# One planned list of steps for an attention stage, with four blocks of the next matrix product placed among the steps

## The chip, the cores and the metric

The kernel runs on one core of one Trainium2 chip. The metric is the device time of one execution in microseconds (us). It is given as the median of several runs. One more execution was recorded by the hardware profiler, and every row below comes from that one.

The engines carry short names. PE is TensorE, whose matmuls and weight loads (PEld) overlap. DVE is VectorE, ACT is ScalarE, POOL is GpSimd, and SP is SyncE, which here only issues DMAs. Each engine runs its own instructions in the order in which they were written, and waits at an instruction whose inputs or buffers are not ready.

## What is computed

The reference is a causal attention followed by two feed-forward layers:

```python
scores = (q @ k^T) / sqrt(64)            # batch 2, heads 12, seq 448, head_dim 64
scores = where(mask, -1e9, scores)
attn = exp(scores - max); attn /= sum(attn) + 1e-9
x = (attn @ v) as [896, 768]
h = x @ w_in                             # 768 -> 2048
g = h if h >= 1, 0 if h <= -1, else (h + 1)**2 / 4
x = g @ w_out                            # 2048 -> 768
...                                      # then one of 8 experts per token: relu(x @ w1[e]) @ w2[e], gated
```

`w_in` and `w_out` come as 64-bit floats, and the kernel turns them into 32-bit ones on the chip.

## The kernel before

**Stages.** The 24 heads are worked on as 12 pairs, pairs 0 to 5 for batch 0 and pairs 6 to 11 for batch 1. Each pair fills one of the six 128-row pieces of `xh["x", b]` and `xl["x", b]`, the high and low part of the attention's output. Then comes the first layer (`gemm1`): 16 blocks `m` of 128 output features, for two batches. A block is six triples of matmuls (`mm3`, L102 to L104), so 18 matmuls of 448 columns. The second layer (`gemm2`) and an expert follow, built from the same triples.

**Steps of a pair.** `m` is the head of the pair (0 or 1) and `i`, `j` a block of 112 rows or columns.

- S (`t_S`, L178, PE): scores of block `i`, one matmul for each head, into two "s" banks of PSUM.
- K (`t_K`, L194, DVE): adds the mask and takes the row maximum.
- E (`t_E`, L198, ACT): exponential with row sums.
- SUM (`t_SUM`, L205 and L206, DVE): the reciprocal of the row sums, for both heads at once.
- N (`t_N`, L211, POOL): multiplies a block by the reciprocal.
- F (`t_F`, L221, PE): transposes of 112x112, four, three or three of them into a "t" bank.
- T (`t_T`, L228, ACT): copies that bank to SBUF.
- V (`t_V`, L235, PE): probabilities times values, into the "x" bank.
- XH and XL (L242, L246, DVE): high part, and low part, of the pair's output.

**Order.** `ORDER` is a table for one turn of a loop. `S:3@0` is a step of the turn's own pair, `T:21@2` one of the pair two turns back. The loop runs 15 turns, so in the last ones fewer and fewer pairs have steps left. `FILL` and `PREP` put work of the first layer among the last turns: three blocks of batch 0 (`EARLY = 3`) and the preparation of their weights.

**Preparing a weight** (`from64` and `work`, tiles of 128x768): Abs on ACT (L92), four DVE operations, called Z1 (L93), Z2 (L95), C1 (L96) and C2 (L98) here, then the high part H on ACT (L132) and the low part L on POOL (L133). In `gemm1` this goes on beside the matmuls, two weights ahead (`Ahead.step`). What follows a block's matmuls is `act1`: a clip on DVE (L272), a square on ACT (L273), a maximum on DVE (L275), a high part on ACT and a low part on POOL.

**Buffers.** [...] The raw weights have two buffers, the raw q and k three.

Of the kernel before, what the change touches and what calls it, by code (L numbers as in the profile page):

```python
# [28 lines left out]
SIGN = 0x80000000  # L29
# [2 lines left out]

ORDER = [(t.split("@")[0], int(t.split("@")[1])) for t in """
    SUM@1 XL@3 F:00@2 S:3@0 S:2@0 K:31@0 N:30@1 K:30@0 K:20@0 T:21@2 T:01@2 N:20@1 F:10@2 T:00@2 K:21@0 E:31@0
    E:30@0 N:10@1 E:20@0 F:11@2 E:21@0 F:20@1 V:0@2 V:2@2 T:11@2 S:1@0 S:0@0 K:11@0 N:31@1 K:10@0 V:3@2 T:10@2
    K:00@0 T:20@1 E:11@0 E:10@0 N:21@1 K:01@0 V:1@2 N:01@1 E:00@0 N:11@1 XH@2 F:21@1 F:01@1 E:01@0 N:00@1
""".split()]
VB = 3 + max(lag for _, lag in ORDER)  # L40
LAST_V = max((lag, n, int(t[2:])) for n, (t, lag) in enumerate(ORDER) if t[:1] == "V")[2]

FILL = {(1, 'F:11'): 3, (1, 'V:1'): 3}
PREP = {(-1, 'F:10'): 1, (-1, 'V:0'): 1, (-1, 'F:21'): 1, (0, 'F:00'): 1, (0, 'F:11'): 1, (0, 'V:0'): 1, (0, 'V:1'): 1, (1, 'F:00'): 1, (1, 'F:11'): 1}
EARLY = 3
BANKS = {"s": 4, "t": 3, "x": 1}
CYCLE = "ststsxst"


def f32(ap):  # L50
    return ap.bitcast(F32)
# [3 lines left out]
def routed_block(ctx, tc, qk, v, w_in, w_out, w_g, w1, w2, out):  # L55
    nc = tc.nc
# [104 lines left out]

    at = ExitStack()
    aq = at.enter_context(tc.tile_pool(name="aq", bufs=2))
    raw_qk, val, hilo, pr, pt, px, pss, pst = {}, {}, {}, {}, {}, {}, {}, {}

    def t_load(p):
        raw_qk[p] = aq.tile([P, 2, S], F32, tag="qk", name="qk", bufs=3)
        nc.sync.dma_start(raw_qk[p], qk[p])
        val[p] = aq.tile([C, 2, NB, D], F32, tag="v", name="v", bufs=VB)
        nc.sync.dma_start(val[p], v[p])  # L170
# [7 lines left out]
            pe.matmul(ps[:, :w], raw_qk[p][r, 0, C * i:w], raw_qk[p][r, 1, :w], start=True, stop=True)  # L178

    def stats(p):  # L180
        if p not in pr:
            pr[p] = (
                [aq.tile([C, TRI[NB]], F32, tag="pr", name="pr", bufs=6) for m in range(2)],
                aq.tile([C, 2, NB], F32, tag="nm", name="nm", bufs=4),
                aq.tile([C, 2, NB], F32, tag="sm", name="sm", bufs=4),
            )
        return pr[p]
# [60 lines left out]
    STEPS = {n[2:]: f for n, f in locals().items() if n.startswith("t_")}  # L248

    def evac(ps, a, c):  # L250
        act.copy(a, ps)
        dve.tensor_tensor(c, ps, f32(a), op=ALU.subtract)


    def new_g(pool_, b, q):
        for hl, d in (("h", gh), ("l", gl)):
            d[b, q] = pool_.tile([P, 4, S], F32R, tag=f"g{hl}{b}{q}", name=f"g{hl}")

    def g_of(d, b, k):
        return d[b, k // 4][:, k % 4]  # L260

    def gemm1(m, b, wt, ps):

        wh, wl = wt
        for k in range(KD):
            mm3(ps, wh[:, k], wl[:, k], xh["x", b][:, k], xl["x", b][:, k], k == 0, k == KD - 1)
            yield

    def act1(m, b, ps, step):

        u = ga.tile([P, S], F32, tag="u", name="u")
        dve.tensor_scalar(u, ps, -1.0, 1.0, op0=ALU.max, op1=ALU.min)  # L272
        act.activation(u, u, AF.Square, bias=half, scale=0.5)  # L273
# [186 lines left out]
    ws = Ahead(win + wout)  # L460

    with tc.manual_schedule():
        dve.memset(half, 0.5)
# [12 lines left out]
        for q in range(1):
            new_g(g0, 0, q)
        N = NP

        held, banks = [], []  # L480

        def early():

            for m in range(EARLY):
                while not ws.ready:
                    ws.step(EARLY)
                held.append(ws.take())
                banks.append(bank("s"))
                yield from gemm1(m, 0, held[m], banks[m])

        fill = early()
        t_load(0)
        t_load(1)
        for s in range(N + max(lag for _, lag in ORDER)):
            if s + 2 < N:
                t_load(s + 2)
            for name, lag in ORDER:
                if 0 <= s - lag < N:
                    step, _, at_ = name.partition(":")
                    STEPS[step](s - lag, *(int(c) for c in at_))  # L500
                    for _ in range(FILL.get((s - N, name), 0)):
                        next(fill, None)
                    for _ in range(PREP.get((s - N, name), 0)):
                        ws.step(EARLY - len(held))
            if s == 2:
                load_gates()
            if s == N - 4:
                ws.load()
        for _ in fill:
            pass  # L510
# [131 lines left out]
```

## Time and profile before

| | |
|---|---|
| median of 3 runs | 480.35 us (480.21 to 480.82) |
| the profiled execution's own time | 480.02 us |
| its span, first to last instruction | 478.0 us |
| mean granted TensorE clock | 0.984 |
| busy: PE, DVE, ACT, POOL | 459.4, 266.5, 195.4, 199.7 us |
| the chain that ended last | PE 91%, DVE 4%, POOL 2%, ACT 1%, DMA 1% |

A matmul's end is modelled, and matmuls overlap in the pipeline. A PE that is shown busy is therefore not a PE at its best pace. How many instructions it starts in a stretch says more, and so does the granted clock beside it. The difference between the execution's time and its span, 2.0 us, is taken as fixed.

### The profile page before, as it was taken

How to read it: one execution, taken by the hardware profiler on the slowest of the kernel's cores; microseconds unless marked ns; L12 is line 12 of the kernel's file. 1: busy time of each engine (PE TensorE's matmuls, PEld its weight loads, DVE VectorE, ACT ScalarE, POOL GpSimd, SP SyncE). 2: the span in 40 equal slices, each digit the busy share in tenths (PEclk: the TensorE clock that was granted, in tenths of full speed). 3: DMA queues.
4: the chain of work that ended last, by engine and by line, in shares of the span. 5: the costliest groups of instructions: out<-in, count | busy, mean ns of one | idle time of the engine just before them, and what ended most of it. 6: DMA issues, size and time to landing. Idle time of an engine off the chain costs nothing.

```text
span 478.0 us, 6657 instructions
## 1 busy us (share of the span) xinstructions
PE 459.4 (96%) x2422; PEld 389.8 (82%) x2422; DVE 266.5 (56%) x538; ACT 195.4 (41%) x455; POOL 199.7 (42%) x190
## 2 busy tenths in 40 slices
PE   5999999679999999999999999999999999999995
PEld 3666565448889999999999999999978999999994
DVE  3576776843699999999947648366111441111111
ACT  4689889742445545545323223232132322211100
POOL 1645654761457677686514133141141222232210
PEclk9999999769999999999999999999999999999999
DMA  6332270240232432322315324150032110123311
GB/s 190 103 117 84 92 248 1 66 133 0 67 123 77 132 114 84 133 80 96 123 55 177 88 89 141 40 171 1 11 122 66 35 55 25 64 82 107 100 60 43
DMA packets 13093, 43.00 MB, mean 90 GB/s; under 512 B 1600, under 2 KB 3264, under 8 KB 13056
## 3 DMA queue, kind: packets, MB, share of 16 engines
q1 hardware_dynamic: 13056, 42.52, 27.6%
q8 instruction: 21, 0.34, 0.3%
q14 instruction: 16, 0.13, 0.1%
HBM read 39.76 MB, written 2.75 MB: 89 GB/s over the span
## 4 chain that ended last, share of the span: by engine, by line
PE 91%; DVE 4%; POOL 2%; ACT 1%; DMA 1%; issue 0%; DVEq 0%; ACTq 0%
PE ps L102 12%; PE ps L104 12%; PE ps L103 12%; PE pt L102 9%; PE pt L104 9%; PE pt L103 9%; PE ps L178 7%; PE pt L221 5%; PE px L235 5%; PE px L103 3%; PE px L104 3%; PE px L102 3%; DVE ps L194 1%; POOL pr L211 1%; DVE wc L98 1%; POOL wlo L133 1%
## 5 line engine op out<-in xcount | busy, mean ns | idle before, releaser
L133 POOL TENSOR_TENSOR wlo<-wc,whi 128x768 fp32r<-128x768 f32 (+1 forms) x34 | 67.6, 1987 | 108.5 <-ACT whi L132 70.5
L133 POOL TENSOR_TENSOR wlo<-wraw,whi 128x512 fp32r<-128x512 f32 (+1 forms) x20 | 30.2, 1513 | 92.0 <-ACT whi L132 80.3
L211 POOL TENSOR_SCALAR pr<-pr,sm 112x224 f32<-112x224 f32 (+2 forms) x96 | 50.5, 547 | 42.7 <-DVE sm L206 42.6
L277 POOL TENSOR_TENSOR gl<-u,gh 128x448 fp32r<-128x448 f32 x32 | 50.7, 1598 | 15.6 <-ACT gh L276 15.6
L102 PE MATMUL ps<-xh,whi 128*128 128x448 f32 x150 | 55.8, 372 | 0.0
L104 PE MATMUL ps<-xh,wlo 128*128 128x448 f32 x150 | 55.3, 368 | 0.4 <-POOL wlo L133 0.4
L103 PE MATMUL ps<-xl,whi 128*128 128x448 f32 x150 | 55.3, 369 | 0.0
L198 ACT ACTIVATE pr<-ps,nm 112x448 f32<-112x448 f32 (+3 forms) x96 | 46.5, 510 | 16.4 <-DVE nm L194 12.6
L194 DVE CUSTOM_DVE_ANT_0 ps<-ps,mask 112x448 f32<-112x448 f32 (+3 forms) x96 | 40.3, 481 | 23.1 <-PE ps L178 23.1
L132 ACT CAST whi<-wc 128x768 fp32r<-128x768 f32 (+1 forms) x34 | 27.2, 799 | 60.6 <-DVE wc L98 59.8
L96 DVE TENSOR_SCALAR wc<-wc 128x768 f32<-128x768 f32 (+1 forms) x34 | 44.4, 1306 | 0.8
L221 PEld LDWEIGHTS pt<-ident,pr 112*112 112x112 f32 x240 | 26.6, 148 | 20.1 <-POOL pr L211 9.9
L178 PE MATMUL ps<-qk 64*112 64x448 f32 (+3 forms) x192 | 37.6, 489 | 5.0 <-DMA qk<-qk 4.0
L273 ACT ACTIVATE u<-u,half 128x448 f32<-128x448 f32 x32 | 21.4, 669 | 48.0 <-DVE u L272 48.0
L95 DVE SCALAR_TENSOR_TENSOR wz<-wraw,wz 128x768 uint32<-128x768 uint32 (+1 forms) x34 | 40.2, 1182 | 0.6
L221 PE MATMUL pt<-ident,pr 112*112 112x112 f32 x240 | 33.1, 291 | 7.0 <-POOL pr L211 7.0
L102 PE MATMUL pt<-xh,whi 128*128 128x448 f32 x102 | 37.4, 367 | 0.0
L104 PE MATMUL pt<-xh,wlo 128*128 128x448 f32 x102 | 37.4, 366 | 0.0
L103 PE MATMUL pt<-xl,whi 128*128 128x448 f32 x102 | 37.3, 366 | 0.0
L98 DVE SCALAR_TENSOR_TENSOR wc<-wc,wz 128x768 uint32<-128x768 uint32 (+1 forms) x34 | 36.4, 1069 | 0.7
L178 PEld LDWEIGHTS ps<-qk 64*112 64x112 f32 x192 | 21.0, 196 | 17.8 <-ACT pr L198 5.7
L102 PE MATMUL ps<-gh,whi 128*128 128x448 f32 x96 | 35.3, 368 | 0.0
(159 smaller groups left out, 972.9 us busy)
## 6 DMA issues: line engine op xcount, KB each, us to landing
wraw<-w_in SPq DMA_DIRECT2D x16, 768.0 KB, 4.4
wraw<-w_out SPq DMA_DIRECT2D x12, 640.0 KB, 4.0
qk<-qk SPq DMA_DIRECT2D x12, 448.0 KB, 3.8
wraw<-w_out SPq DMA_DIRECT2D x6, 768.0 KB, 4.6
wraw<-w SPq DMA_DIRECT2D x8, 384.0 KB, 3.0
wraw<-w SPq DMA_DIRECT2D x12, 256.0 KB, 2.5
v<-v SPq DMA_DIRECT2D x12, 224.0 KB, 4.0
out<-res SPq DMA_DIRECT2D x11, 224.0 KB, 2.0
```

The costliest lines, as they stand in the source:

```text
L96: dve.tensor_scalar(c, c, 2.0**-31, None, op0=ALU.max)
L98: dve.scalar_tensor_tensor(cu, cu, 3, z, op0=ALU.logical_shift_left, op1=ALU.bitwise_xor)
L102: pe.matmul(ps, wh, xh, start=start, stop=False)
L103: pe.matmul(ps, wh, xl, start=False, stop=False)
L104: pe.matmul(ps, wl, xh, start=False, stop=stop)
L133: pool.tensor_tensor(fl, v, f32(fh), op=ALU.subtract)
L178: pe.matmul(ps[:, :w], raw_qk[p][r, 0, C * i:w], raw_qk[p][r, 1, :w], start=True, stop=True)
L194: dve.tensor_tensor_reduce(z, z, mask[:, S - w:], -0.125, 3.0e38, ALU.add, ALU.min, nm[:, m, i:i + 1])
L198: act.activation(q[m][:, TRI[i]:TRI[i + 1]], pss.pop((p, i, m))[:, :C * (i + 1)], AF.Exp, bias=nm[:, m, i:i + 1], scale=-1.0, accum_out=sm ...
L211: pool.tensor_scalar(r, r, sm[:, m, i:i + 1], 0.0, op0=ALU.mult, op1=ALU.add)
L221: pe.transpose(ps[:, o:o + C], q[:, TRI[i] + C * j:TRI[i] + C * j + C], ident[:C, :C])
L277: pool.tensor_tensor(g_of(gl, b, m), u, f32(g_of(gh, b, m)), op=ALU.subtract)
```

## The change

1. `ORDER` is now one list of every step of every pair, run once from first to last. `S2/7` is step S of block 2 for pair 7; `G1.4` is triple 4 of block 1 of the first layer.
2. Four blocks of the first layer for batch 0 (`EARLY = 4`) stand in the list as single triples `Gm.k`. Each `Gm.k` needs pair `k` only. Six triples make a block. All four blocks use one new PSUM bank "f", and "t" has two banks instead of three.
3. The weights of these four blocks are prepared in halves of 384 columns by steps of the list: A (Abs, ACT), Z1, Z2, C1, C2 (DVE), H (ACT), L (POOL). The first two prepared weights lie in the space of `g` tiles that are needed late (`hold`). The raw weights are loaded by the steps LW.
4. The clip, square, maximum, high and low part of these four blocks are steps too: U1 (DVE), SQ (ACT), U2 (DVE), GH (ACT), GL (POOL).
5. SUM is done for each head by itself.
6. The gates' weights are loaded after the first layer instead of in the third turn of the attention.

```diff
-ORDER = [(t.split("@")[0], int(t.split("@")[1])) for t in """
-    SUM@1 XL@3 F:00@2 S:3@0 S:2@0 K:31@0 N:30@1 K:30@0 K:20@0 T:21@2 T:01@2 N:20@1 F:10@2 T:00@2 K:21@0 E:31@0
...
-FILL = {(1, 'F:11'): 3, (1, 'V:1'): 3}
...
-EARLY = 3
-BANKS = {"s": 4, "t": 3, "x": 1}
-CYCLE = "ststsxst"
+ORDER = """
+    LQ/0 LW/0 S2/0 S3/0 K21/0 LQ/1 K20/0 E21/0 K30/0 E20/0 K31/0 E30/0 S1/0 E31/0 K11/0 LW/1 K10/0 E11/0 Z11/0
...
+    V3/11 XH/11 GH/3 XL/11 GL/3
+""".split()
+EARLY, HOLD, SPARE, VB = 4, 2, 4, 5
+BANKS = {"s": 4, "t": 2, "x": 1, "f": 1}
+CYCLE = "stsfstsx"
...
-    def t_SUM(p):
-        sm = pr[p][2]
+    def t_SUM(p, _, m):
+        sm = sms[p][:, m]
         dve.tensor_scalar_add(sm, sm, 1e-9)
         dve.reciprocal(sm, sm)
...
+    def t_A(j, h):
...
+        act.activation(ec[j][:, E * h:E * (h + 1)], words(j, h)[1].bitcast(F32), AF.Abs, scale=2.0**-16)
+
+    def t_Z(j, n, h):
+        low, high = words(j, h)
+        if n == 1:
...
+            dve.tensor_scalar(ez[j, h], low, 29, SIGN, op0=ALU.logical_shift_right, op1=ALU.bitwise_xor)
+        else:
+            z = ez[j, h]
+            dve.scalar_tensor_tensor(z, high, SIGN, z, op0=ALU.bitwise_and, op1=ALU.bitwise_xor)
+
+    def t_C(j, n, h):
+        c = ec[j][:, E * h:E * (h + 1)]
+        if n == 1:
+            dve.tensor_scalar(c, c, 2.0**-31, None, op0=ALU.max)
+        else:
+            cu = c.bitcast(U32)
+            dve.scalar_tensor_tensor(cu, cu, 3, ez.pop((j, h)), op0=ALU.logical_shift_left, op1=ALU.bitwise_xor)
...
+    def t_G(m, k):
+        if k == 0:
+            ebank[m] = bank("f" if m < SPARE else "s")
+        wh, wl = held[m]
+        mm3(ebank[m], wh[:, k], wl[:, k], xh["x", 0][:, k], xl["x", 0][:, k], k == 0, k == KD - 1)
...
-        t_load(0)
-        t_load(1)
-        for s in range(N + max(lag for _, lag in ORDER)):
...
+        for token in ORDER:
...
+            STEPS[name](*([] if p is None else [int(p)]), *args)
+        ws.load()
         at.close()
...
-        for m in range(EARLY):
-            act1(m, 0, banks[m], lambda: None)
         for m in range(KF):
...
+                    ahead = 1 if m < HOLD else 2
+                    act1(m, b, ps, lambda: ws.step(ahead))
...
+        load_gates()
```

**PE at the end of the attention.** The order before, from the transposes of pair 10 on (`pt<-ident,pr` is F, `px<-pt,v` is V, `xh,whi` the first layer):

```order
L221 MATMUL pt<-ident,pr 112x112 x20
L235 MATMUL px<-pt,v 64x448 x2
L235 MATMUL px<-pt,v 64x224 x2
L235 MATMUL px<-pt,v 64x112 x2
L235 MATMUL px<-pt,v 64x336 x2
L221 MATMUL pt<-ident,pr 112x112 x17
L102 MATMUL ps<-xh,whi 128x448
L103 MATMUL ps<-xl,whi 128x448
L104 MATMUL ps<-xh,wlo 128x448
```

The same place now, from the last transposes of pair 10 (`pf` is the new bank):

```order
L251 MATMUL pt<-ident,pr 112x112 x4
L133 MATMUL pf<-xh,whi 128x448
L134 MATMUL pf<-xl,whi 128x448
L135 MATMUL pf<-xh,wlo 128x448
L251 MATMUL pt<-ident,pr 112x112 x3
L266 MATMUL px<-pt,v 64x448 x2
L266 MATMUL px<-pt,v 64x224 x2
L266 MATMUL px<-pt,v 64x336 x2
L266 MATMUL px<-pt,v 64x112 x2
L251 MATMUL pt<-ident,pr 112x112 x3
L133 MATMUL pf<-xh,whi 128x448
L134 MATMUL pf<-xl,whi 128x448
```

Before, 37 transposes and the V of pair 10 stood ahead of the first triple. Now a triple stands after every three to four transposes, down to pair 11's own.

**DVE early in the attention.** The order before, from one SUM on (`ps,nm<-ps,mask` and `nm` are the two records of one K):

```order
L205 TENSOR_SCALAR sm<-sm 112x8
L206 RECIPROCAL sm<-sm 112x8
L246 TENSOR_TENSOR xl<-px,xh 128x448
L194 ISA ps,nm<-ps,mask 112x448
L194 ISA nm 112x1
L194 ISA ps,nm<-ps,mask 112x448
L194 ISA nm 112x1
```

The place now, in the steps around pair 2:

```order
L236 RECIPROCAL sm<-sm 112x4
L315 SCALAR_TENSOR_TENSOR wc<-wc,ez 128x384
L273 CAST xh<-px 128x448
L222 ISA ps,nm<-ps,mask 112x224
L222 ISA nm 112x1
L222 ISA ps,nm<-ps,mask 112x224
L222 ISA nm 112x1
L304 TENSOR_SCALAR ez<-wraw 128x384
L222 ISA ps,nm<-ps,mask 112x112
L222 ISA nm 112x1
```

Halves of the weights' preparation (`wc`, `ez`) now stand between the K steps, in front of steps for which ACT and then PE wait.

## Rows read from the trace of the kernel before

**Rows 1.** Windows: us, busy by engine, then clock, DMA share, GB/s; the attention's end.

```profile
84.00:96.00 12.00, 8.03 (x55) 5.69 (x55) 10.58 (x28) 8.21 (x25) 8.98 (x11) 0.78 0.21 67
96.00:108.00 12.00, 8.61 (x40) 5.90 (x37) 5.03 (x7) 5.57 (x11) 7.59 (x7) 0.65 0.42 131
```

**Rows 2.** Windows, the columns of rows 1: attention, first layer, expert.

```profile
24.30:82.36 58.06, 58.06 (x446) 35.52 (x445) 42.10 (x173) 51.17 (x188) 30.53 (x64) 1.00 0.34 112
132.00:228.00 96.00, 96.00 (x469) 87.87 (x470) 89.73 (x105) 49.53 (x78) 69.51 (x40) 1.00 0.32 105
...
432.00:456.00 24.00, 24.00 (x120) 22.24 (x119) 3.12 (x5) 3.11 (x5) 6.46 (x5) 1.00 0.31 103
```

**Rows 3.** Chain that ended last: start, us, what; one full pair.

```profile
47.92 1.50 PE ps L178 x8
49.43 1.01 PE pt L221 x9
50.43 1.28 PE px L235 x8
51.71 0.89 PE ps L178 x7
52.60 1.01 PE px L235 x8
53.61 1.20 PE pt L221 x11
54.81 1.50 PE ps L178 x8
```

**Rows 4.** Waits of PE: us in total, times, longest.

```profile
PE pt L221 <- POOL pr L211: 7.0, 4, 4.0
PE ps L104 <- POOL wlo L133: 0.4, 1, 0.4
```

**Rows 5.** Timeline of PE at the attention's end: start, us, instruction.

```profile
110.70 0.47 PE L102 MATMUL ps<-xh,whi 128*128 128x448 f32 x1
```

**Rows 6.** Chain that ended last, the start: pairs 1 and 2.

```profile
10.30 3.38 PE ps L178 x8
18.71 2.89 PE ps L178 x8
21.60 1.43 PE pt L221 x9
```

**Rows 7.** Groups of ACT by form, 82 to 110 us: busy, mean ns, idle before.

```profile
L92 ACT ACTIVATE wc<-wraw 128x768 f32<-128x768 f32 x3 | 2.8, 942 | 0.0
L132 ACT CAST whi<-wc 128x768 fp32r<-128x768 f32 x3 | 2.5, 833 | 3.2 <-DVE wc L98 3.2
```

**Rows 8.** Groups of DVE by form, 82 to 110 us: busy, mean ns, idle before.

```profile
L95 DVE SCALAR_TENSOR_TENSOR wz<-wraw,wz 128x768 uint32<-128x768 uint32 x3 | 3.2, 1065 | 0.0
L98 DVE SCALAR_TENSOR_TENSOR wc<-wc,wz 128x768 uint32<-128x768 uint32 x3 | 2.9, 965 | 0.1
L93 DVE TENSOR_SCALAR wz<-wraw 128x768 uint32<-128x768 uint32 x3 | 2.0, 652 | 0.0
L96 DVE TENSOR_SCALAR wc<-wc 128x768 f32<-128x768 f32 x3 | 1.6, 545 | 0.0
```

**Rows 9.** The same groups, 168 to 228 us, in the first layer.

```profile
L95 DVE SCALAR_TENSOR_TENSOR wz<-wraw,wz 128x768 uint32<-128x768 uint32 x8 | 12.3, 1532 | 0.0
L96 DVE TENSOR_SCALAR wc<-wc 128x768 f32<-128x768 f32 x8 | 12.0, 1506 | 0.0
L98 DVE SCALAR_TENSOR_TENSOR wc<-wc,wz 128x768 uint32<-128x768 uint32 x8 | 11.0, 1371 | 0.0
L93 DVE TENSOR_SCALAR wz<-wraw 128x768 uint32<-128x768 uint32 x7 | 3.8, 545 | 0.0
```

**Rows 10.** Groups of DVE, 24 to 82 us: the second instruction of SUM.

```profile
L206 DVE RECIPROCAL sm<-sm 112x8 f32<-112x8 f32 x8 | 1.6, 203 | 0.3
```

**Rows 11.** Source L205 over the whole run: ns min/median/max.

```profile
L205 DVE TENSOR_SCALAR sm<-sm x12: 164/172/1472, 11.4 to 91.1; 112x8 f32<-112x8 f32 x12
```

More of the change, by code (lines that the diff above doesn't have):

```diff
@@ L180, in stats @@
     def stats(p):
[L181 to L187, printed above, removed]
+        if p not in nms:
+            nms[p] = aq.tile([C, 2, NB], F32, tag="nm", name="nm", bufs=4)
+            sms[p] = aq.tile([C, 2, NB], F32, tag="sm", name="sm", bufs=4)
+        return nms[p], sms[p]
     def t_K(p, i, m):
-        nm = stats(p)[1]
+        nm = stats(p)[0]
         w = C * (i + 1)
@@ L196, in t_E @@
     def t_E(p, i, m):
-        q, nm, sm = stats(p)
+        nm, sm = stats(p)
+        if (p, m) not in pr:
+            pr[p, m] = aq.tile([C, TRI[NB]], F32, tag="pr", name="pr", bufs=6)
         act.activation(
-            q[m][:, TRI[i]:TRI[i + 1]], pss.pop((p, i, m))[:, :C * (i + 1)], AF.Exp,
+            pr[p, m][:, TRI[i]:TRI[i + 1]], pss.pop((p, i, m))[:, :C * (i + 1)], AF.Exp,
             bias=nm[:, m, i:i + 1], scale=-1.0, accum_out=sm[:, m, i:i + 1],
         )
-    def t_SUM(p):
-        sm = pr[p][2]
+    def t_SUM(p, _, m):
+        sm = sms[p][:, m]
         dve.tensor_scalar_add(sm, sm, 1e-9)
@@ L208, in t_N @@
     def t_N(p, i, m):
-        q, nm, sm = pr[p]
-        r = q[m][:, TRI[i]:TRI[i + 1]]
+        sm = sms[p]
+        r = pr[p, m][:, TRI[i]:TRI[i + 1]]
         pool.tensor_scalar(r, r, sm[:, m, i:i + 1], 0.0, op0=ALU.mult, op1=ALU.add)
@@ L215, in t_F @@
     def t_F(p, g, m):
-        q = pr[p][0][m]
+        q = pr[p, m]
         ps = pst[p, g, m] = bank("t")[:C]
@@ L232, in t_V @@
         if p not in px:
-            px[p] = bank("x")
+            px[p], parts[p] = bank("x"), 0
+        parts[p] += 1
         for m in range(2):
@@ L236, in t_V @@
                 px[p][D * m:D * m + D, C * j:], val[p][:, m, j],
-                pt[p, m][:, COL[j]:COL[j] + S - C * j], start=(j == 0), stop=(j == LAST_V),
+                pt[p, m][:, COL[j]:COL[j] + S - C * j], start=(j == 0), stop=(parts[p] == NB),
             )
@@ L246, in t_XL @@
         dve.tensor_tensor(xl["x", b][:, h], px[p], f32(xh["x", b][:, h]), op=ALU.subtract)
-    STEPS = {n[2:]: f for n, f in locals().items() if n.startswith("t_")}
     def evac(ps, a, c):
@@ L252, in evac, with t_LW, words, e_halves @@
         dve.tensor_tensor(c, ps, f32(a), op=ALU.subtract)
+    eraw, ec, ez, ew = {}, {}, {}, {}
+    E = KD * P // 2
+    def t_LW(j):
+        eraw[j] = wp.tile([P, 12 * P], F32, tag="wraw", name="wraw", bufs=2)
+        nc.sync.dma_start(eraw[j].bitcast(I64).rearrange("p (k f) -> p k f", f=P), w_in[j])
+    def words(j, h):
+        w = eraw[j][:, 2 * E * h:2 * E * (h + 1)].rearrange("p (n two) -> p n two", two=2).bitcast(U32)
+        return w[:, :, 0], w[:, :, 1]
+    def t_A(j, h):
+        if j not in ec:
+            ec[j] = wp.tile([P, 6 * P], F32, tag="wc", name="wc", bufs=2)
+        act.activation(ec[j][:, E * h:E * (h + 1)], words(j, h)[1].bitcast(F32), AF.Abs, scale=2.0**-16)
+    def t_Z(j, n, h):
+        low, high = words(j, h)
+        if n == 1:
+            ez[j, h] = aq.tile([P, E], U32, tag=f"ez{h}", name="ez", bufs=1)
+            dve.tensor_scalar(ez[j, h], low, 29, SIGN, op0=ALU.logical_shift_right, op1=ALU.bitwise_xor)
[9 more added lines that the diff above has]
+            dve.scalar_tensor_tensor(cu, cu, 3, ez.pop((j, h)), op0=ALU.logical_shift_left, op1=ALU.bitwise_xor)
+    held = {}
+    def e_halves(j, h):
+        if j not in ew:
+            if j < HOLD:
+                ew[j] = [t.rearrange("p a s -> p (a s)")[:, KD * P * j:KD * P * (j + 1)] for t in hold]
+                held[j] = [t.rearrange("p (k f) -> p k f", f=P) for t in ew[j]]
+            else:
+                held[j] = [wp.tile([P, 6, P], F32R, tag=g, name=g, bufs=3) for g in ("whi", "wlo")]
+                ew[j] = [t.rearrange("p k f -> p (k f)") for t in held[j]]
+        return [t[:, E * h:E * (h + 1)] for t in ew[j]]
+    def t_H(j, h):
+        act.copy(e_halves(j, h)[0], ec[j][:, E * h:E * (h + 1)])
+    def t_L(j, h):
+        hi, lo = e_halves(j, h)
+        pool.tensor_tensor(lo, ec[j][:, E * h:E * (h + 1)], f32(hi), op=ALU.subtract)
     def new_g(pool_, b, q):
@@ L262, in gemm1, with clip1, act1 @@
     def gemm1(m, b, wt, ps):
-        wh, wl = wt
         for k in range(KD):
-            mm3(ps, wh[:, k], wl[:, k], xh["x", b][:, k], xl["x", b][:, k], k == 0, k == KD - 1)
-            yield
-    def act1(m, b, ps, step):
+            mm3(ps, wt[0][:, k], wt[1][:, k], xh["x", b][:, k], xl["x", b][:, k], k == 0, k == KD - 1)
+    def clip1(ps):
         u = ga.tile([P, S], F32, tag="u", name="u")
         dve.tensor_scalar(u, ps, -1.0, 1.0, op0=ALU.max, op1=ALU.min)
+        return u
+    def act1(m, b, ps, step):
+        u = clip1(ps)
         act.activation(u, u, AF.Square, bias=half, scale=0.5)
@@ L278, in act1, with t_U, t_SQ, t_GH @@
         step()
+    ebank, eu = {}, {}
+    def t_G(m, k):
[3 more added lines that the diff above has]
+        mm3(ebank[m], wh[:, k], wl[:, k], xh["x", 0][:, k], xl["x", 0][:, k], k == 0, k == KD - 1)
+    def t_U(m, n):
+        if n == 1:
+            eu[m] = clip1(ebank[m])
+        else:
+            dve.tensor_tensor(eu[m], ebank[m], eu[m], op=ALU.max)
+    def t_SQ(m):
+        act.activation(eu[m], eu[m], AF.Square, bias=half, scale=0.5)
+    def t_GH(m):
+        act.copy(g_of(gh, 0, m), eu[m])
+    def t_GL(m):
+        pool.tensor_tensor(g_of(gl, 0, m), eu[m], f32(g_of(gh, 0, m)), op=ALU.subtract)
     def gemm2(n, last=None):
@@ L459, in routed_block @@
     wout = [(w_out[n, :, k0:k0 + nk], nk, True) for n in range(KD) for k0, nk in KSUB]
-    ws = Ahead(win + wout)
+    ws = Ahead(win[EARLY:] + wout)
+    STEPS = {n[2:]: f for n, f in locals().items() if n.startswith("t_")}
     with tc.manual_schedule():
@@ L474, in routed_block @@
             new_x(("x", b))
[L476 to L482, printed above, removed]
-            for m in range(EARLY):
[L485 to L491, printed above, removed]
-        t_load(0)
-        t_load(1)
-        for s in range(N + max(lag for _, lag in ORDER)):
[L495 to L510, printed above, removed]
+        new_g(g0, 0, 0)
+        hold = [g0.tile([P, 4, S], F32R, tag=f"g{hl}13", name="hold") for hl in "hl"]
+        for token in ORDER:
+            step, p = token.split("/") if "/" in token else (token, None)
+            name = step.rstrip("0123456789.")
+            args = [int(c) for c in step[len(name):].replace(".", "")]
+            STEPS[name](*([] if p is None else [int(p)]), *args)
+        ws.load()
         at.close()
@@ L515, in gs_of @@
         def gs_of(b, q):
-            return g0 if (b, q) == (0, 0) else gs
+            return g0 if (b, q) in ((0, 0), (1, 3)) else gs
         for q in range(4):
             for b in range(B):
-                if (b, q) != (0, 0):
+                if (b, q) not in ((0, 0), (1, 3)):
                     new_g(gs, b, q)
-        for m in range(EARLY):
-            act1(m, 0, banks[m], lambda: None)
         for m in range(KF):
             wt = held[m] if m < EARLY else ws.take()
-            held[m:m + 1] = [None]
+            held[m] = None
             for b in range(B):
@@ L530, in routed_block @@
                     ps = psum()
-                    for _ in gemm1(m, b, wt, ps):
-                        pass
-                    act1(m, b, ps, ws.step)
+                    gemm1(m, b, wt, ps)
+                    ahead = 1 if m < HOLD else 2
+                    act1(m, b, ps, lambda: ws.step(ahead))
                     if b:
-                        ws.step()
+                        ws.step(ahead)
+            if m == HOLD:
+                new_g(g0, 1, 3)
+        load_gates()
         for b in range(B):
```

47 lines of the change are left out of this document (39 added, 8 removed).

## The prediction

> **What bounds the kernel now.** I read the chain that ended last first: PE holds 91% of it, so the question is where PE loses time. The windows answer that. In the middle of the attention, and from the first layer on, PE is busy throughout at full clock [rows 2], and its waits come to a few microseconds in all [rows 4]. The loss lies at the attention's two ends.
>
> At its end, from 84 to 108 us, PE is busy for 8.0 and 8.6 of 12 us, and the granted clock is 0.78 and 0.65 [rows 1]. POOL's normalised probabilities are late there: 7.0 us of waits in four places, the longest 4.0 [rows 4]. [...]
>
> Between the ends one pair takes 6.89 us (47.92 to the next 1.50 us piece at 54.81) without a gap in the chain: S 1.50 + 0.89 = 2.39, F 1.01 + 1.20 = 2.21, V 1.28 + 1.01 = 2.29 [rows 3]. So 58.06 us are 8.43 pairs, and a pair costs DVE 42.10 / 8.43 = 4.99 us, ACT 6.07 and POOL 3.62 [rows 2]. PE is the bound there, ACT the next.
>
> **The change part by part.** I compare both kernels at one point of PE's work: all twelve pairs and the first 72 matmuls of the first layer (four blocks of batch 0) issued.
>
> *Before.* The attention's last V has been issued when the first layer's tenth matmul starts, at 110.70 [rows 5]. The other 63, at 96 / 469 = 0.205 us [rows 2], are done by 110.7 + 12.9 = 123.6 us.
>
> *Now, start.* The first scores wait for the same first load. The list puts pair 1's scores and all 20 transposes of pair 0 ahead of pair 2's scores; before there were 14. Those scores started at 18.71 [rows 6]. Six more transposes, at half the pace of nine in 1.01 [rows 3], cost some 1.2 us: 20 us. The extra raw weight between pair 0's and pair 1's loads on the SP queue is hidden by the time until pair 1's scores, at 10.30 [rows 6]; without that cover it would cost its own transfer.
>
> *Now, the rest.* From there PE has S of ten pairs (23.9), F of eleven (24.3), V of twelve (27.5) and 72 matmuls at 0.205 (14.8): 90.5 us. The list changes more often between kinds of work, 97 times from there on, where the pieces above already hold 66 runs. Nine transposes take 1.01 and eleven 1.20 [rows 3], so 0.095 each and 0.15 for a run. A change costs between nothing and 0.15; I take 0.1, as a run's 0.15 holds its first start too. 31 of them are 3.1. PE would be through at 20 + 90.5 + 3.1 = 113.6 us.
>
> *Low clock at the start.* It lasts to about 22: the run of nine at 21.60 still took 1.43 [rows 6]. Two microseconds at half pace cost 1.0.
>
> *Waits from the preparation.* This is the uncertain term. Pairs 2 to 7 hold 24 of the 32 half operations on DVE (three weights' worth), and six SUMs more, at 0.20 and 0.17 us [rows 10, 11]: 2.2 us. A weight's four operations cost 1.07 + 0.97 + 0.65 + 0.55 = 3.23 us at the attention's end [rows 8], but 1.53 + 1.51 + 1.37 + 0.55 = 4.95 in the first layer [rows 9]. Cut in halves they add 12 instructions here, at most 0.17 each: 2.0. DVE then needs 6 x 4.99 + 2.2 + 9.7 = 41.8 us, or up to 49.0 with the upper figures. PE needs 6 x 6.89, six triples (3.7) and some 2 for changes: 47.0. ACT needs 36.4, and for A and H about three and four weights' worth at 0.94 and 0.83 [rows 7], 42.5. Behind each half on DVE's queue stand K steps; their E, and then the bank for the next S, come later. DVE is at 89 to 104% of PE's time. The low end leaves PE no reason to wait; I take 2.2 us, nearer to it, since POOL is busy for 30.53 of 58.06 us here [rows 2], less than the 69.51 of 96 behind the upper figures.
>
> What lies behind them shows in SUM's first instruction: eight elements take 0.17 us and once 1.47 [rows 11]; C1 takes 0.55 or 1.51 [rows 8, 9]. [...]
>
> *End.* Pair 11's last transposes wait for eight N, now with twelve triples' fill among PE's own steps (G2.4 to G3.5 and pair 10's V). Pair 11 needs S to K, E, SUM and N, some 8 us if a pair's E and N on ACT and POOL follow one another; PE has 9 x 0.61 us of triples and 2.2 + 2.3 of transposes and V to issue meanwhile. I cost the remaining wait at nothing; if the fill fell short, part of the 7.0 [rows 4] would stay.
>
> *Work that leaves the next stage.* The three `act1` of the early blocks, and a fourth, are gone from the first layer, and a fourth weight is ready: the 0.4 us that PE waited for `wlo` [rows 4] go. The gates' load now stands on DVE ahead of the second layer; its results are needed after that layer, and two weights are ready by then: nothing. Two "t" banks instead of three would bite through T on ACT, which is in the waits above.
>
> **The sum.** 113.6 + 1.0 + 2.2 = 116.8 against 123.6: 6.8 us, and 0.4: 7.2. From the profiled 480.02 that gives 472.8 us. The median shown is 480.35, so the same sum from there gives 473.1; the difference is a tenth of what is at stake.
>
> **The rivals.**
>
> 1. *DVE becomes the bound in pairs 2 to 7.* For it: the upper figures. DVE's 49.0 us, at the 89.73 of 96 it reaches in the first layer [rows 2], take 52.4, 5.4 more than PE's 47.0. 113.6 + 1.0 + 5.4 = 120.0, a gain of 4.0: 476.0 us. Against it: POOL's lower load.
> 2. *The list runs without waits.* 113.6 with full clock from 20 us on: a gain of 10.4, 469.6 us. For it: every engine but PE has spare time by the lower figures.
> 3. *Slower: the clock falls inside the list.* Where PE waited for a third of the time, its granted clock fell to 0.78 and 0.65, 0.715 on average [rows 1]. If waits behind DVE bring that about over pairs 2 to 7, their 47.0 us become 65.7: 18.7 more, 491 us. It decides from about 19 us of PE work at such a clock, which costs the 7.2 gained. Against it: the clock held 1.00 through 58 us of the same kinds of work [rows 2]. [...]
> 4. *The first layer gives it back.* DVE is busy for 89.73 of 96 us there [rows 2]. If weights come late after the list, PE waits for them instead, and the end stays: about 480 us. Against it: four blocks of batch 1 come first, with their weights ready.
>
> **How the numbers follow.** Likeliest 0.62; rivals 0.20, 0.11, 0.04 and 0.03, in this order. Some 0.2% is what a measurement of this kernel can tell from no change. The first three cases are faster, 0.93; rival 4 is the same, 0.03; rival 3 slower, 0.04. After the attention some 1080 matmuls are left; the pitch was 0.205 in the first layer and 0.200 in the expert [rows 2], with nothing in the rows that says why, so the rest may move by 2.5 us, half of the 5 between them, either way. The range takes in rivals 1 and 2 with part of that: 467.5 to 478.0. Predicted: 472.8.
>
> **What would show it.** Right: the chain ends with almost no POOL in it around the attention's end, the clock stays at 1.00 from about 22 us on, the waits of F for POOL fall from 7.0 to below 2, and the first matmul of batch 1 in the first layer starts at about 117 us. Waits of S for ACT, of 2 to 5 us in all between 20 and 70 us, would be the term of the preparation; Z2, C1 and C2 halves of over 0.7 us would be rival 1. Windows with a clock below 1.00 after 25 us would be rival 3. A wait for `whi` or `wlo` after 117 us would be rival 4. Wrong would be the sum if pair 2's scores start after 22, or if the point comes before 112 us or after 121.

## The result, and the profile after

The changed kernel takes 464.96 us (median of 4 runs, 464.19 to 466.12) against 480.36 us (480.21 to 480.82) in the same session. The ratio is 0.968, with an interval of 0.966 to 0.970. That is 15.4 us faster, twice the 7.2 us forecast, and below the predicted range of 467.5 to 478.0. The profiled execution is the slowest of the four, 466.12 us with a span of 464.4. The ratios in this document leave out an execution that took over 1.5% longer than the fastest of its kernel, which is one each of x1, x2 and x9 below.

The page of the kernel after: the span, busy times, and PE and its granted clock in 40 slices.

```profile
span 464.4 us, 6693 instructions
PE 451.5 (97%) x2422; PEld 384.0 (83%) x2422; DVE 269.7 (58%) x578; ACT 198.2 (43%) x463; POOL 194.8 (42%) x194
PE   5999999999999999999999999999999999999994
PEclk9999999999999999999999999999999999999998
```

PE's busy time fell by 7.9 us (459.4 before), its idle time by 5.7 (478.0 - 459.4 = 18.6, now 12.9). Part of the old busy time was work at half the clock: before, from 105 to 107 us, PE was busy for 2.00 of 2.00 us with 10 matmuls at a granted clock of 0.50. The windows show the difference, with the columns of [rows 1]. The first two answer to [rows 1]; the last two are pairs 2 to 7 and pairs 8 to 11.

```profile
84.00:96.00 12.00, 12.00 (x95) 8.35 (x91) 8.29 (x32) 9.79 (x33) 7.35 (x15) 1.00 0.00 1
96.00:108.00 12.00, 12.00 (x87) 9.03 (x85) 5.00 (x17) 7.77 (x22) 4.94 (x9) 1.00 0.00 1
...
19.98:65.43 45.45, 44.24 (x332) 28.22 (x331) 42.31 (x156) 43.38 (x147) 33.36 (x56) 1.00 0.39 130
65.43:108.81 43.38, 43.38 (x316) 30.30 (x315) 27.04 (x102) 33.15 (x107) 22.40 (x43) 1.00 0.18 64
```

The attention's end is as dense now as its middle was [rows 2]: 12.00 of 12 us busy at a granted clock of 1.00, with 95 and 87 matmuls where there were 55 and 40 [rows 1]. The waits of PE that are left answer to [rows 4]:

```profile
PE ps L209 <- DMA qk<-qk: 4.8, 1, 4.8
PE pt L251 <- POOL pr L241: 0.8, 1, 0.8
PE pt L251 <- ACT pt L258: 0.4, 1, 0.4
```

The 7.0 us of waits for POOL have become 0.8, and the wait for `wlo` is gone. The chain that ended last (start, us, what) shows the pieces that answer to [rows 3] and [rows 6]; lines are left out between them:

```profile
20.05 1.50 PE ps L209 x8
21.55 2.04 PE px L266 x16
...
27.31 1.51 PE ps L209 x8
28.82 2.04 PE px L266 x16
...
98.97 2.07 PE px L266 x16
```

Pair 2's larger scores take 1.50 us at once, not 2.89 [rows 6]. And V of a pair is one run of sixteen matmuls in 2.04 us, where it was two runs of eight in 1.28 + 1.01 = 2.29 [rows 3]. Last, the timeline of PE at the end of the list, which answers to [rows 5] (`xh,hold` is the first layer's batch 1):

```profile
106.77 2.11 PE L266 MATMUL px<-pt,v 112*64 112x448 f32 x16
108.81 0.47 PE L133 MATMUL pt<-xh,hold 128*128 128x448 f32 x1
```

So the point at which the prediction compares the kernels came at 108.81 us, not at 116.8; before it was 123.57. The 14.8 us gained there are all of the gain: the two profiled executions differ by 13.9 us (480.02 - 466.12). From the point to the first layer's 576th matmul it took 103.9 us before and 104.3 now, and another 0.9 us went behind the last matmul. The time outside the span, taken as a fixed 2.0 us, was 1.7 here.

### The profile page after: what moved, and what is told of

Its sections match the earlier page's. It is cut to its first block, busy times and chain, and to the rows that moved or that the text cites. A ratio compares the mean times of both kernels' runs of the same rounds, so it can differ in the third digit from the quotient of the medians.

```text
span 464.4 us, 6693 instructions
## 1 busy us (share of the span) xinstructions
PE 451.5 (97%) x2422; PEld 384.0 (83%) x2422; DVE 269.7 (58%) x578; ACT 198.2 (43%) x463; POOL 194.8 (42%) x194
## 4 chain that ended last, share of the span: by engine, by line
PE 95%; DVE 2%; DMA 1%; POOL 1%; ACT 0%; issue 0%; DVEq 0%; POOLq 0%
PE ps L133 12%; PE ps L135 12%; PE ps L134 12%; PE ps L209 7%; PE pt L133 6%; PE pt L135 6%; PE pt L134 6%; PE pt L251 5%; PE px L266 4%; PE pf L133 4%; PE pf L135 4%; PE pf L134 4%; PE px L133 3%; PE px L135 3%; PE px L134 3%; DMA qk<-qk 1%
## 5 line engine op out<-in xcount | busy, mean ns | idle before, releaser
L241 POOL TENSOR_SCALAR pr<-pr,sm 112x448 f32<-112x448 f32 (+3 forms) x96 | 49.0, 530 | 41.4 <-DVE sm L235 27.9
L228 ACT ACTIVATE pr<-ps,nm 112x224 f32<-112x224 f32 (+3 forms) x96 | 47.0, 504 | 9.4 <-DVE nm L222 9.4
L222 DVE CUSTOM_DVE_ANT_0 ps<-ps,mask 112x336 f32<-112x336 f32 (+3 forms) x96 | 40.7, 475 | 12.0 <-PE ps L209 11.7
L133 PE MATMUL ps<-xh,whi 128*128 128x448 f32 x126 | 46.3, 368 | 0.0
L135 PE MATMUL ps<-xh,wlo 128*128 128x448 f32 x126 | 46.2, 367 | 0.0
L209 PE MATMUL ps<-qk 64*112 64x336 f32 (+3 forms) x192 | 35.9, 473 | 4.9 <-DMA qk<-qk 4.8
L134 PE MATMUL ps<-gl,whi 128*128 128x448 f32 x96 | 35.3, 368 | 0.0
L135 PE MATMUL ps<-gh,wlo 128*128 128x448 f32 x96 | 35.3, 368 | 0.0
L258 ACT COPY pt<-pt 112x336 f32<-112x336 f32 (+1 forms) x72 | 31.8, 483 | 7.8 <-PE pt L251 7.3
L163 ACT CAST whi<-wraw 128x512 fp32r<-128x512 f32 (+1 forms) x20 | 14.1, 703 | 44.2 <-PE pt L134 17.0
```

The source lines that it names most:

```text
L163: act.copy(fh, v)
L228: act.activation(pr[p, m][:, TRI[i]:TRI[i + 1]], pss.pop((p, i, m))[:, :C * (i + 1)], AF.Exp, bias=nm[:, m, i:i + 1], scale=-1.0, accum_ou ...
```

## The experiments

Whole times of one program scatter by 2 to 7 us between executions (x9: 460.55 to 467.66), in part for a reason told at the end. Therefore I read most experiments in a stretch of the profiled execution: from the start of pair 3's larger scores to the point, which is all twelve pairs and 72 matmuls of the first layer issued. Both are starts on PE's timeline. Expectations and some readings below count from pair 2's scores; pair 3's are the better mark, since in some executions the matmuls of pair 2 still ran at half pace (its larger scores took 2.96 us on the timelines of before and of x7, 1.57 on that of the change).

| kernel | median, us (lowest to highest) | ratio to before, interval | pair 3 | point | between |
|---|---|---|---|---|---|
| before | 480.36 (480.21 to 480.82) | | 27.10 | 123.57 | 96.5 |
| after | 464.96 (464.19 to 466.12) | 0.968, 0.966 to 0.970 | 27.24 | 108.81 | 81.6 |
| x9, after again | 463.99 (460.55 to 467.66) | 0.972, 0.967 to 0.978 | 25.61 | 107.50 | 81.9 |
| x1, not filled | 474.07 (469.36 to 476.71) | 0.989, 0.982 to 0.996 | 25.41 | 116.86 | 91.4 |
| x11, list bare | 481.89, one run | | 23.88 | 128.99 | 105.1 |
| x6, before with bare tail | 479.45, one run | | 27.57 | 122.66 | 95.1 |
| x3, whole preparation | 468.61 (467.81 to 469.69) | 0.981, 0.977 to 0.985 | 28.61 | 113.12 | 84.5 |
| x2, V split | 464.80 (463.92 to 472.40) | 0.972, 0.967 to 0.977 | 27.09 | 112.92 | 85.8 |
| x8, grouped | 465.53 (464.13 to 468.15) | 0.973, 0.969 to 0.976 | 26.21 | 109.09 | 82.9 |
| x4, three blocks | 463.81 (461.23 to 466.12) | 0.970, 0.965 to 0.976 | 25.74 | 108.34 | 82.6 |
| x7, loads by need | 465.89 (462.55 to 467.83) | 0.975, 0.972 to 0.978 | 28.91 | 110.38 | 81.5 |
| x5, before, V joined | 490.94 (489.77 to 492.91) | 1.026, 1.022 to 1.031 | 25.30 | 132.69 | 107.4 |
| x10, before, V between | 483.73 (483.07 to 485.32) | 1.012, 1.007 to 1.016 | 25.57 | 129.47 | 103.9 |

In the later sessions the kernel before had medians of 478.2 to 478.5. The one program that was profiled twice, the changed one, gives 81.6 and 81.9: differences of under half a microsecond say nothing. Every other stretch rests on one trace.

### x1: the list with the preparation, without the early triples

```diff
-    G0.0 T11/2 Z10/2 T21/2 F00/2 Z20/2 E10/3 ...
+    T11/2 Z10/2 T21/2 F00/2 Z20/2 E10/3 ...
...
-                if b or m >= EARLY:
+                if True:
```

All steps G, U1, SQ, U2, GH and GL are taken out, and the four blocks run in the first layer.

> The list as it is, with its early preparation of four weights, but without the steps G, U, SQ, GH and GL: the four blocks of batch 0 are computed behind the attention, with the other blocks. PE's work is the same. Theory A (the triples fill PE while pair 11's probabilities are late, and keep its clock up): the last V comes with gaps ahead of it and the clock falls there once more; 4 to 9 us slower than the change, 469 to 474 us. Rival B (the better order of the steps and the preparation moved away from the attention's end bring the gain, the fill is only moved work): within 2 us of the change, 463 to 467 us.

The stretch grows by 9.9 us, of the 14.7 that the 72 matmuls take one after another (102.17 to 116.86). Among the steps of the list they thus cost only 4.8. Without them the list has gaps. F takes 34.6 us from start to start against 23.9 in the changed kernel, and the waits of PE (the columns as in [rows 4]) are many short ones:

```profile
PE pt L248 <- ACT pt L255: 4.9, 14, 0.5
PE ps L206 <- DMA qk<-qk: 4.1, 1, 4.1
PE ps L206 <- ACT pr L225: 1.8, 3, 1.2
PE pt L248 <- POOL pr L238: 1.3, 3, 0.8
PE px L263 <- ACT pt L255: 1.0, 2, 0.7
```

The triples fill waits of F for the copies T on ACT (two "t" banks) and for N. The granted clock stayed at 1.00 from 17 us to the end of this list too. So the triples did not buy the clock. That the absence of long waits did is argued, not shown: from 8 to 14 us of this trace the clock is 0.73 (mean of the execution 0.993, against 0.996 for the change), and the waits of PE ahead of and in that stretch were of 0.2 to 1.2 us.

### x11 and x6: no preparation and no triples, in either order

```diff
-EARLY, HOLD, SPARE, VB = 4, 2, 4, 5
+EARLY, HOLD, SPARE, VB = 0, 0, 4, 5
```

That is x11, whose list keeps the attention's steps alone.

> The list with the attention's steps alone: no preparation, no triples; all 32 blocks of the first layer come behind it, the first weights with no cover. Compared with the kernel before without its tail's preparation, whose last V was at 97.6 us. Theory A (the order of the attention's steps itself is better): the last V at 93 to 96 us. Rival B (the order alone brings nothing, room for the preparation and the triples is what it gives): 97 to 102 us. The total time is 478 to 486 us either way, as 72 matmuls more and the first preparation come behind.

```diff
-FILL = {(1, 'F:11'): 3, (1, 'V:1'): 3}
-PREP = {(-1, 'F:10'): 1, (-1, 'V:0'): 1, ...
+FILL = {}
+PREP = {}
```

That is x6, the kernel before with nothing but attention in its last turns.

> The kernel before, with no preparation and no triples in its last turns; the three early blocks come after the attention. Theory A (the preparation stands on DVE, ACT and POOL in front of pair 11's steps and makes its probabilities late): the last V comes 4 to 8 us earlier than 110.3 us, with less waiting for POOL ahead of it. Rival B (pair 11's own chain is that long): the last V stays within 2 us. The total time can go either way, as PE then waits for the first weight behind the attention.

Alone, the old order is the faster one: from pair 3's scores to the end of V it takes 70.2 us in x6 (27.57 to 97.8), the list 75.3 in x11 (23.88 to 99.19), as rival B had it. The order as such brings no gain. One thing is not taken apart: x11 keeps two "t" banks and leaves "f" empty during the attention, and F waits 4.3 us there for T on ACT. How fast the bare list runs with a third "t" bank no run shows. What the preparation in the last turns cost is now plain: 83.6 us before (27.10 to 110.70) against 70.2, so 13.4, of which only 1.8 are the nine matmuls that ran there. That is more than theory A allowed: the last V starts at 95.93 instead of 108.66. But x6 as a whole is no faster than before. Waits of PE, and its timeline after the attention:

```profile
PE ps L102 <- ACT whi L132: 5.2, 1, 5.2
PE ps L178 <- DMA qk<-qk: 4.4, 1, 4.4
PE ps L104 <- POOL wlo L133: 1.7, 2, 1.3
PE ps L178 <- ACT pr L198: 1.0, 2, 0.6
PE pt L221 <- POOL pr L211: 0.6, 1, 0.6
```

```profile
103.21 0.74 PE L102 MATMUL ps<-xh,whi 128*128 128x448 f32 x1 [5.17 <-ACT whi L132]
...
106.51 0.57 PE L103 MATMUL ps<-xl,whi 128*128 128x448 f32 x1
106.89 0.57 PE L104 MATMUL ps<-xh,wlo 128*128 128x448 f32 x1
```

F's waits for POOL are 0.6 us here, not 7.0 [rows 4]. In their place PE waits 5.2 us for the first weight and then issues at 0.37 us a matmul, the pitch that the trace of before has at a granted clock of 0.50 (106.22 to 106.96 us); the window of x6 from 96 to 108 us has a granted clock of 0.73. In the old order the weights came late, or the attention did.

### x3: the preparation in whole operations

```diff
-    E = KD * P // 2
+    E = KD * P
```

Each weight has one A, Z1, Z2, C1, C2, H and L, at the place of the second half.

> The change, with each preparation step done once over 768 columns, at the place of its second half. Theory A (DVE and ACT have room enough beside PE, halves are not what keeps PE fed): within 1 us of the change. Rival B (whole operations of 0.5 to 1 us on DVE ahead of K steps make S, and then PE, wait): 3 to 6 us slower, 468 to 471 us, with waits of S for ACT in the trace.

The stretch grows by 2.9 us and the median by 3.6 over that of the change. The waits of the scores' weight loads for ACT grow, after above and x3 below:

```profile
PEld ps L209 <- ACT pr L228: 3.7, 9, 1.4
```

```profile
PEld ps L206 <- ACT pr L225: 5.3, 12, 1.4
```

A whole Z2 (0.95 us) delays the K behind it on DVE, then E, then the banks of the next scores. N on POOL takes longer as well, by 0.70 us beside a whole operation at the most, by 0.49 beside a half (the last section shows such places). The halves are worth about 3 us, with the later place of the first half's work, which x3 changes too. I had counted only their cost, 2.0 us on DVE.

### x2, x5 and x10: V of a pair in one run

```diff
-    V2/6 N20/7 V1/6 E30/8 K31/8 N11/7 V3/6 N01/7 GH/0 G1.0 XH/6
+    V2/6 N20/7 E30/8 K31/8 N11/7 N01/7 GH/0 G1.0 V1/6 V3/6 XH/6
```

That is x2: in each pair V1 and V3 stand behind the next step of another kind on PE.

> The change, with the four V of a pair in two runs on PE instead of one, another step of PE between them, as before the change. Theory A (a run of V in one piece saves PE 0.25 us for each pair, as 2.04 against 2.29 us in the two traces): about 2.5 to 3 us slower than the change, 467.5 to 468 us. Rival B (the difference is only where waits are booked): within 0.7 us of the change, 464.3 to 465.7 us.

```diff
-    ... F:20@1 V:0@2 V:2@2 T:11@2 S:1@0 S:0@0 ... V:3@2 T:10@2 K:00@0 ... K:01@0 V:1@2 N:01@1
+    ... F:20@1 T:11@2 S:1@0 S:0@0 ... T:10@2 K:00@0 ... K:01@0 V:0@2 V:2@2 V:3@2 V:1@2 N:01@1
```

That is x5, the old order with V together in the second place.

> The kernel before, with the four V of a pair in one run on PE, at the place of the last. Theory A (a run in one piece saves 0.25 us for each pair): the pair's pitch goes from 6.89 to about 6.65 us and the time falls by 2 to 3 us, to about 477.5 to 478.5 us. Rival B (ACT sets the pitch of 6.89 us): the time stays within 0.7 us of 480.4 us.

```diff
-    ... F:20@1 V:0@2 V:2@2 T:11@2 ... V:3@2 T:10@2 ... V:1@2 N:01@1 ... XH@2
+    ... F:20@1 V:0@3 V:2@3 V:1@3 V:3@3 T:11@2 ... T:10@2 ... N:01@1 ... XH@3
```

That is x10, with V together between the larger and the smaller scores, one turn later.

> The kernel before, with the four V of a pair in one run, one turn later, between the large and the small scores of the next pairs, where the change's list has them. Theory A (a run in one piece saves 0.25 us for each pair, if it stands where S would otherwise wait for E): the pitch of the pairs goes from 6.89 to 6.6 to 6.7 us, and the time falls by 1 to 2.5 us. Rival B (ACT's E and T set the pitch): 6.85 us or more, and the time does not fall.

Split, V takes 24.7 us in the stretch, against 22.4 joined, S 22.3 against 21.0, the triples 17.9 against 16.9, and the stretch grows by 4.2 us. The median of x2 does not show that; it lies in rival B's range. Its profiled execution ran the rest at the quicker of the two paces told of below, as x9's did, and those two differ by 4.9 us (465.49 and 460.55). So this rests on one trace of x2. In the old order V joined also takes 2.04 us, but each time something else comes late, and both kernels become slower, which neither theory A allowed. The chain of one pair in x5:

```profile
50.97 1.48 ACT pr L198 x5
...
53.40 0.45 PE ps L178 x2
53.85 2.04 PE px L235 x16
55.89 1.20 PE pt L221 x11
```

ACT's E holds the chain there, and a pair costs 7.92 us instead of 6.89. The weight loads that wait, in x5 and then in x10:

```profile
PEld ps L178 <- ACT pr L198: 16.5, 47, 1.9
```

```profile
PEld pt L221 <- POOL pr L211: 14.9, 12, 5.0
```

In x10 it is F that waits for N, and a pair costs 7.23 us. The saving of 0.25 us a pair showed only in the list, where PE has other steps during those waits.

### x8 and x4: how the triples are placed, and how many

```diff
-    GH/0 G1.0 XH/6 ... K00/8 G1.1 K01/8 ... E11/8 G1.2 E00/8
+    GH/0 XH/6 ... K00/8 G1.0 G1.1 G1.2 K01/8 ... E11/8 E00/8
```

That is x8: blocks 1 and 2 in runs of three triples.

> The change, with the triples of blocks 1 and 2 in runs of three instead of one by one: eight runs fewer on PE. Theory A (a change between kinds of work costs PE about 0.1 us, as a triple alone takes 0.70 us and one in a run 0.61): 0.8 to 1.6 us faster, 463.4 to 464.2 us. Rival B (single triples fill waits for T that would otherwise show): no faster, up to 2 us slower.

```diff
-EARLY, HOLD, SPARE, VB = 4, 2, 4, 5
+EARLY, HOLD, SPARE, VB = 3, 2, 4, 5
```

That is x4, without block 3 and the preparation of its weight.

> The change with three early blocks: the fourth weight's preparation and block 3 are taken out of the list and done in the first layer. Pair 11's last transposes then have no triples between them. Theory A (fill at the end is what counts): PE waits for POOL or ACT there for 2 to 4 us and the time is 1.5 to 4 us above the change, 466.5 to 469 us. Rival B (pair 11's chain is short enough without it): within 0.7 us of the change.

Grouped, the triples take 0.9 us less (16.0 for 16.9 from start to start), and F 2.2 more (26.1 for 23.9): 1.3 us lost in the stretch. The changes between kinds of work did cost PE something, those 0.9 us, but a triple at the right place filled a wait of F that was worth more. The fourth block is worth 1.0 us in the stretch by x4, and in the medians nothing that can be told.

### x7: the raw weights later, behind the q and k that are needed first

```diff
-    LQ/0 LW/0 S2/0 S3/0 K21/0 LQ/1 K20/0 ...
+    LQ/0 S2/0 S3/0 K21/0 LQ/1 LW/0 K20/0 ...
```

The second raw weight moves behind LQ/2 in the same way.

> The change, with the first raw weight's load behind pair 1's and the second's behind pair 2's, in the order of their use. Theory A (the first scores start at 4.83 us instead of 3.98 because the raw weights' loads share the DMA engines with the first q and k): the first matmul starts near 4.0 us and the time falls by 0.5 to 0.9 us. Rival B (pair 1's chain sets the pace there, or the landing time is another matter): within 0.3 us of the change.

The first matmul started at 4.15 us (4.83 in the trace of the change, 4.01 in x9, which has the loads in the old place), and pair 2's scores at 19.95 (19.98 and 18.11). The first load is not held up by the weight's, and the time shows no gain. The weight's load does stand in front of something: pair 1's q and k land at 7.82 us in x7, at 10.57 in the trace of the change and 10.79 in x9, where PE waits 1.1 us for them. In x7 PE did not wait but worked longer at half pace (pair 2's larger scores took 2.96 us, 1.75 in x9), so what that wait costs stays open.

### x9: the change once more

> The change itself once more, beside the other runs of this call, to see how far its time and the start of its attention move from run to run. All theories: 464 to 466.5 us; from pair 2's first scores to the end of the early blocks 88.8 us, as before, wherever the start lies.

x9 bears out the change's gain in another session (ratio 0.972) and gives the scatter of one stretch, 0.3 us. From pair 2's scores it is 89.4 us, 0.6 more than expected.

## Why the prediction was wrong, point by point

**Right: where the loss lay and what takes it away.** The waits for POOL fell below 2 us (0.8), the clock reads 1.00 in the windows after 25 us, no weight is late after the point, and pair 2's scores started at 19.98 (forecast 20). That last agreement is partly luck: the same program began them at 18.11 in x9.

**Wrong: "Now, the rest", 90.5 + 3.1, and the two terms behind it.** From pair 2's scores to the point the forecast has 96.8 us, the trace 88.8, and the point at 108.81 lies below the 112 us that I had named as the sign of a wrong sum. By kind, from start to start on PE:

| term | forecast | measured |
|---|---|---|
| V of twelve pairs | 27.5 | 24.5 |
| S, F, triples and changes between kinds | 23.9 + 24.3 + 14.8 + 3.1 = 66.1 | 23.5 + 22.7 + 16.9 = 63.2 |
| low clock at the start | 1.0 | 0 |
| waits from the preparation (measured: all waits of F) | 2.2 | 1.2 |

1. *V was priced from its two runs before.* The list issues it in one run. That is 3.0 us, and the order of the steps, which I had, shows it. x5 has V joined at 2.04 us as well, and x2, split again, needs 2.25 a pair.
2. *The changes between kinds were charged on top of prices that held them.* The triples' 14.8 became 16.9, so their changes cost 2.1 of the 3.1. But S and F became cheaper by 0.4 and 1.6 than the pieces of [rows 3]. I had read those as work at its best pace, because PE shows no wait from 24.30 to 82.36 us. Its weight loads do, in the trace of before and that stretch, once in nearly each of the 8.43 pairs (columns as in [rows 4]):

```profile
PEld pt L221 <- ACT pt L228: 3.8, 8, 0.5
...
PEld ps L178 <- ACT pr L198: 2.7, 8, 0.3
...
PEld ps L178 <- ACT pt L228: 1.6, 8, 0.2
```

   That these waits made the pieces longer is argued from these rows; no run separates it.
3. *Low clock and waits.* The term of 1.0 was called a low clock, but the windows of both traces from 8 to 22 us have a granted clock of 1.00. What the traces show there is a pace: eight matmuls of the larger scores in 2.89 us [rows 6], against 1.50 later [rows 3]. What sets it no run shows. On the timeline of this execution it ended at pair 2's scores (1.57), in x7 it lasted through them (2.96, and V at 22.84 still 2.42), so the size of the term differs from run to run.

Three readings in the prediction were wrong without deciding it. DVE's lower figure, 41.8 us, leaves out the 2.0 for the halves that its upper one, 49.0, holds; with them it is 43.8, and the trace has 42.31 of 45.45 us. Not 1080 but 1726 matmuls followed the point; 1080 are those of the two layers. And the raw weight's load, called hidden there, put off pair 1's q and k by some 3 us (x7): in this execution PE did not wait for them, in x9 1.1 us.

**Rival 1 (DVE the bound) was refuted, and my reason for its low chance was wrong.** I leaned to the lower figures because POOL would be less busy than in the first layer. It was not: 33.36 of 45.45 us, 73%, the same as 69.51 of 96 [rows 2]. Still the halves took by their medians what the lower figures say (source lines of Z1, Z2, C1, C2: ns min/median/max):

```profile
L304 DVE TENSOR_SCALAR ez<-wraw x8: 330/356/897, 10.1 to 56.5; 128x384 uint32<-128x384 uint32 x8
L307 DVE SCALAR_TENSOR_TENSOR ez<-wraw,ez x8: 527/559/1140, 11.1 to 57.4; 128x384 uint32<-128x384 uint32 x8
L312 DVE TENSOR_SCALAR wc<-wc x8: 351/434/636, 12.3 to 60.7; 128x384 f32<-128x384 f32 x8
L315 DVE SCALAR_TENSOR_TENSOR wc<-wc,ez x8: 526/541/715, 15.4 to 61.4; 128x384 uint32<-128x384 uint32 x8
```

What differs is how long the one POOL instruction is that DVE meets: an N takes 0.36 to 0.64 us, `gl` and `wlo` in the first layer 1.4 to 2.2. That this length counts, and not how long POOL is busy, is my reading of the rows of the last section; no run varied it alone.

**Rivals 2 to 4.** The list came nearest to rival 2 (no waits, 469.6 us) and beat it by the terms 1 and 2, which it shared. No window of the list after 25 us has a clock below 1.00 (rival 3), and the first layer gave back 0.3 us (rival 4).

**Where the 15 us come from.** From pair 3's scores to the point:

| | before | after |
|---|---|---|
| attention alone | 70.2 (x6) | 75.3 (x11) |
| preparation of weights (before with nine matmuls) | 13.4 | 1.5 (x1 less x11: 76.8 - 75.3) |
| the 72 matmuls (before the other 63) | 12.9 | 4.8 |
| together | 96.5 | 81.6 |

The gain is made twice: the preparation lies in pairs 0 to 7, where it costs 1.5 us and not in front of pair 11's K, E and N, and the triples lie in gaps that the list has anyway. The order by itself, with two "t" banks, loses 5 us of that. The split goes by one sequence of steps, the order first, then the preparation, then the triples. The forecast's mechanism was right, its sizes were not. No variant is clearly faster than the change: the medians of x4 and x9 lie inside each other's spread.

## What to carry to other kernels

Price a step by the run in which the new order issues it, and read the waits of weight loads beside those of the matmuls before calling a stretch of PE free of slack. Work that feeds a later stage belongs early, in small pieces, where its engines have room; the matmuls that it frees belong singly into the gaps behind transposes. An order that is worse by itself can be the better one once such work fills it, so test the order bare, and each filling alone. And when an engine's results come late, hold each of its instructions against the same one elsewhere in the trace: it may have taken longer itself, as N did (1.44 us for 0.36), and not only have queued.

## What the runs showed of the hardware that was not expected

**The same stream of triples has two paces.** Windows of 200 us in the first and second layer, columns as in [rows 1], of the change and then of x9, the same program:

```profile
120.00:320.00 200.00, 200.00 (x970) 181.66 (x969) 153.95 (x182) 79.16 (x120) 97.72 (x56) 1.00 0.31 99
```

```profile
120.00:320.00 200.00, 200.00 (x989) 185.38 (x987) 151.18 (x179) 78.57 (x120) 98.96 (x56) 1.00 0.31 99
```

970 or 989 matmuls, so 0.206 or 0.202 us each, at the same granted clock and with nothing in the rows that says why. The other traces of the list with its early weights had one or the other (969 or 970 in x3, x4 and x8, 988 or 989 in x1, x2 and x7). From the point to the last matmul it is worth 4.2 us (348.5 or 344.2), all of it over the 1080 matmuls of the two layers, which is part of why whole times of one program scatter. The cause stays open. The kernel before was profiled at the slower pace, as the change was, so the comparison of the two traces is fair.

**Where DVE and POOL met, the one or the other took longer.** Three places in the trace of the kernel before: N beside Z2 and C1, C1 beside `gl`, and SUM beside `wlo` (timelines: start, us, instruction), then N of the same size in the middle of the attention (busy, mean ns, idle):

```profile
100.43 1.08 DVE L95 SCALAR_TENSOR_TENSOR wz<-wraw,wz 128x768 uint32<-128x768 uint32 x1
100.68 1.44 POOL L211 TENSOR_SCALAR pr<-pr,sm 112x112 f32<-112x112 f32 x1
101.43 0.55 DVE L96 TENSOR_SCALAR wc<-wc 128x768 f32<-128x768 f32 x1
...
168.12 1.86 POOL L277 TENSOR_TENSOR gl<-u,gh 128x448 fp32r<-128x448 f32 x1
168.90 1.50 DVE L96 TENSOR_SCALAR wc<-wc 128x768 f32<-128x768 f32 x1
...
90.76 1.81 POOL L133 TENSOR_TENSOR wlo<-wc,whi 128x768 fp32r<-128x768 f32 x1 [2.89 <-ACT whi L132]
91.12 1.47 DVE L205 TENSOR_SCALAR sm<-sm 112x8 f32<-112x8 f32 x1 [1.31 <-ACT pr L198]
...
L211 POOL TENSOR_SCALAR pr<-pr,sm 112x112 f32<-112x112 f32 x16 | 5.7, 359 | 0.0
```

N takes 0.36 us in the middle of the attention; here it started during Z2, took 1.44 and ended 0.14 us behind C1, which took its usual 0.55. Beside `gl`, C1 took 1.50 (with POOL idle 0.56, x6 at 100.74); it started during `gl` and ended 0.4 us behind it. SUM's first instruction takes 0.17 us [rows 11]; here it took 1.47, started during `wlo` and ended with it. That the longer one was held up by the other engine's is my reading of these times; what holds it up no run shows.

So the preparation in the last turns did not only stand in front of pair 11's steps on their queues. From 84 us on, SUM took 1.3 us longer (1.47 for 0.17), and the N took 4.6 us longer in all than the same sizes in the middle of the attention, and two of PE's four waits for POOL [rows 4] ended with the N of 100.68 and of the next one. In x6, without the preparation there, no N took over 0.65 us. What part of the 13.4 us this is, no run separates.
